# Attention, balanced mixture and routed mixture on one core: small pieces of work dealt out at another spacing among the matrix products

## The chip, the core and the metric

The kernel runs on one core of a Trainium2 chip. The metric is device time in microseconds (us), the median of three runs. The engines of the core work side by side, each through its own instructions in program order: TensorE (PE in the profile), VectorE (DVE), ScalarE (ACT), GpSimd (POOL) and SyncE (SP), whose queue issues most of the DMAs. They wait for each other on semaphores.

## The reference

Three layers follow each other. An attention reads 32 state rows per head and writes both ways (x reads the states, the states read x); its 2176 rows of 512 go into a mixture of eight experts whose weights come from an exponential that is balanced eight times over rows and columns (the Sinkhorn steps); the result goes into a second mixture in which each row takes one expert.

```python
P = np.exp(logits - logits.max())                    # logits = x @ w_gate, 2176 x 8
for _ in range(8):
    P /= P.sum(1, keepdims=True) + 1e-09
    P /= P.sum(0, keepdims=True) + 1e-09
    P *= N / E
for e in range(E):
    out += P[:, e:e+1] * (np.maximum(x @ w1[e], 0.0) @ w2[e])
```

The second mixture picks the largest logit of each row, computes relu(x @ w1[e]) @ w2[e] for the rows of expert e, and scales them by a softmax weight and a sigmoid.

## The kernel before

Everything is float32 in and out; each product is made of three products of a high and a low half (names ending in h and l, hi and lo), and the low half is the difference of the source and its rounded high half.

**The order is written by hand.** The whole program is traced under a manual schedule: each engine executes what concerns it in the order in which the Python code emits it. So a piece of work that is emitted between two groups of products stands there on TensorE too, and if its operand is late, TensorE waits with everything behind it.

**The balanced mixture** is the bulk: three passes over the rows (PASSES: 768, 768 and 640 rows), and in each 32 steps, one for each of eight experts and four quarters of the hidden width (NU = 32, NQ = 4). A step has two halves. `mm1` (L453) makes seven products of six matmuls each by a Strassen-like scheme: seven operands of x (`xop`, written by `xsums` and `xsplit` at the start of a pass) against seven of the weights (`prep_w1`, on ACT and POOL). Its results are added up on DVE, go through relu on ACT, and are split on ACT and DVE into HB. `mm2` (L519) multiplies them tile by tile (6 tiles of 128 rows, 5 in the last pass) with the second weights, six matmuls a tile, and DVE adds each tile, scaled by its balanced weight, to `acc`. The loop emits mm1 of step s and then mm2 of step s-1. In pass 0 the first two experts are added up without their weights, expert 0 in acc and expert 1 in xst (L531 to L539), because the balanced weights PG are not yet there; at step 8 both are brought together with PG (L540 to L543).

**The side work** is dealt out by a queue: `pump(dt)` (L935) is called after each group of six products with 1.04 us (mm1; 0.88 in the last pass) and after each tile of mm2 with 1.36 us, adds that to a credit of at most four paces, and takes one piece off the queue for each `pace` of credit; `flush` (L931) takes all. The queue holds, in pass 0, the attention of batches 2 and 3 (`window`, L947, and the `lag` pieces; 52 pieces with the gates), the logits (`gate`, L292: per row tile of 128, four products of two matmuls each with 8 columns), and the 18 pieces of `sinkhorn` (L311): each `row` has five instructions on DVE, each `col` a matmul of ones (L337) and four on DVE. The attention of batches 0 and 1 (c1 to c5, named A0, A1, C0 and C1 at the top level) stands ahead of the first product.

**At a pass change** (L1057 to L1068) the x operands of the next pass are split in `todo` pieces behind the tiles of the last two mm2, and each finished tile of acc is stored, transposed on TensorE (`final_a`, L552, matmuls pf) and multiplied with the second mixture's gates (`final_b`, L571, matmuls pl). The routing of finished tiles (`route`, L586: fa, fb and fc, matmuls prank; `sel_a` to `sel_c`, matmuls ptab and pgat) is queued at the beginning of the next pass. At the end of the last pass the first weights of the second mixture are split in eight pieces (`split_piece`, L768), and blocks 0 and 1 of it run (`m1`, `hT`, `m2s`) with the last routing among them (L1147 to L1160); the other blocks follow, each with its weights loaded (`load_w`) and split (`split_w`) when the expert changes.

**Banks.** All results of TensorE go to eight rotating banks of PSUM (`bank`, L72). A bank is free again when its readers on DVE or ACT are done, so a late DVE stops TensorE some tiles later.

## Time and profile before

| | us |
|---|---|
| median of 3 runs | 1878.95 |
| the runs | 1878.01 to 1881.89 |
| the profiled execution, its own time | 1879.49 |
| its span, from the first instruction to the last | 1877.8 |
| TensorE busy | 1804.5 |
| VectorE, GpSimd, ScalarE busy | 1211.8, 1099.3, 653.3 |

The span is 1.7 us shorter than the execution's own time, and that execution is 0.5 us over the median. TensorE counts as busy also when its clock is granted at half; the clock has a row of its own in the page's slices. A wait of an engine is listed with the engine and the line that ended it. Where a POOL or DVE instruction is long without more work in it, the same shape elsewhere tells its usual duration.

### The profile page before, as it was taken

What the parts mean: (1) busy time and instruction counts of PE and PEld (TensorE: products, weight loads), DVE (VectorE), ACT (ScalarE), POOL (GpSimd) and SP (SyncE); (2) the same over time, 40 slices, a digit from 0 to 9 for tenths busy, and PEclk for the clock granted to TensorE, in tenths of its full rate; (3) what the DMA queues carried; (4) which work ended last, traced back from release to release, by engine and by line L of the source; (5) the groups of instructions that cost most, each with busy time, mean ns of one, the idle gap of its engine ahead of it and who ended that gap; (6) DMA issues with size and microseconds to landing.
All of it is one profiled execution on the core that took longest, in us unless ns stands there. A gap on an engine that the chain in (4) does not pass through costs nothing.

```text
span 1877.8 us, 25502 instructions
## 1 busy us (share of the span) xinstructions
PE 1804.5 (96%) x9327; PEld 1607.7 (86%) x9327; DVE 1211.8 (65%) x2041; ACT 653.3 (35%) x1114; POOL 1099.3 (59%) x857
## 2 busy tenths in 40 slices
PE   7998899999999999999999999799999999899998
PEld 5997788999999889999999998689999899778886
DVE  5664769666666676666666666896666666745332
ACT  3432222333333333333333333333333343345333
POOL 2432456666776566666667765577787877412212
PEclk8799899999999999999999999899999999999999
DMA  4243112322222222222222222232222222245122
GB/s 113 74 107 96 51 45 68 102 68 68 68 68 68 90 80 71 70 71 96 68 68 68 68 67 84 67 129 81 80 79 79 90 79 68 76 137 199 62 81 89
DMA packets 126618, 154.65 MB, mean 82 GB/s; under 512 B 41424, under 2 KB 91600, under 8 KB 123920
## 3 DMA queue, kind: packets, MB, share of 16 engines
q1 hardware_dynamic: 121920, 142.41, 24.2%
q0 software_dynamic: 3280, 10.23, 1.7%
q8 instruction: 75, 1.23, 0.3%
q14 instruction: 63, 0.52, 0.1%
q10 hardware_dynamic: 1280, 0.26, 0.1%
HBM read 138.99 MB, written 14.42 MB: 82 GB/s over the span
## 4 chain that ended last, share of the span: by engine, by line
PE 74%; DVE 9%; issue 9%; DMA 5%; POOL 2%; ACT 1%; SPq 0%; POOLq 0%; DVEq 0%; ACTq 0%
PE py L527 12%; PE py L528 12%; PE py L529 12%; PE p L465 11%; PE p L467 11%; PE p L466 11%; DMA out_dram<-xst,si 4%; DMA out_dram<-y,si 1%; DVE HB L478 1%; PE psg L303 1%; PE psr L281 1%; PE pss L206 1%; PE pl L576 1%; DVE acc L547 1%; PE pso L243 1%
## 5 line engine op out<-in xcount | busy, mean ns | idle before, releaser
L443 POOL TENSOR_TENSOR wl<-rawb,wh 128x1024 fp32r<-128x1024 f32 x96 | 230.8, 2405 | 473.1 <-ACT wh L442 473.1
L465 PE MATMUL p<-XR 128*128 128x384 f32 (+1 forms) x1344 | 447.9, 333 | 4.2 <-ACT XR L390 2.8
L467 PE MATMUL p<-XR 128*128 128x384 f32 (+1 forms) x1344 | 444.1, 330 | 4.1 <-POOL XR L432 3.0
L466 PE MATMUL p<-XR 128*128 128x384 f32 (+1 forms) x1344 | 443.7, 330 | 0.9 <-DVE XR L392 0.9
L527 PE MATMUL py<-wh,HB 128*128 128x512 f32 x1088 | 431.6, 397 | 2.4 <-DVE acc L547 2.3
L528 PE MATMUL py<-wl,HB 128*128 128x512 f32 x1088 | 429.0, 394 | 0.0
L529 PE MATMUL py<-wh,HB 128*128 128x512 f32 x1088 | 428.6, 394 | 0.0
L547 DVE SCALAR_TENSOR_TENSOR acc<-py,PG,acc 128x512 f32<-128x512 f32 x485 | 338.9, 741 | 79.3 <-PE py L529 78.7
L432 POOL TENSOR_TENSOR XR<-sst,XR 128x1024 fp32r<-128x1024 f32 x96 | 255.0, 2656 | 50.8 <-ACT XR L426 50.8
L465 PEld LDWEIGHTS p<-XR 128*128 128x128 f32 x1344 | 256.8, 191 | 11.3 <-ACT XR L390 4.1
L467 PEld LDWEIGHTS p<-XR 128*128 128x128 f32 x1344 | 256.5, 191 | 5.4 <-POOL XR L432 3.8
L466 PEld LDWEIGHTS p<-XR 128*128 128x128 f32 x1344 | 256.7, 191 | 4.9 <-DVE XR L392 1.5
L478 DVE SCALAR_TENSOR_TENSOR HB<-u,HB 128x384 fp32r<-128x384 f32 (+1 forms) x192 | 169.3, 883 | 117.4 <-ACT HB L474 117.2
L529 PEld LDWEIGHTS py<-wh,HB 128*128 128x128 f32 x1088 | 206.7, 190 | 44.2
L527 PEld LDWEIGHTS py<-wh,HB 128*128 128x128 f32 x1088 | 206.8, 190 | 44.0 <-DVE acc L547 3.0
L528 PEld LDWEIGHTS py<-wl,HB 128*128 128x128 f32 x1088 | 206.6, 190 | 39.7
L483 ACT COPY u<-p 128x384 f32<-128x384 f32 (+1 forms) x96 | 44.3, 461 | 527.6 <-PE p L467 523.5
L428 POOL TENSOR_TENSOR XR<-rawb,XR 128x512 fp32r<-128x512 f32 x96 | 141.6, 1475 | 7.4 <-ACT XR L422 7.4
L426 ACT CAST XR<-sst 128x1024 fp32r<-128x1024 f32 x96 | 100.8, 1050 | 93.7 <-POOL sst L421 93.7
L474 ACT ACTIVATE HB<-u 128x384 fp32r<-128x384 f32 (+1 forms) x192 | 96.9, 505 | 80.0 <-DVE u L501 72.2
L486 DVE TENSOR_TENSOR u<-p,u 128x384 f32<-128x384 f32 (+1 forms) x96 | 51.3, 534 | 112.6 <-PE p L467 108.2
L474 ACT ACTIVATE HB<-p 128x384 fp32r<-128x384 f32 (+1 forms) x96 | 45.5, 474 | 190.4 <-PE p L467 190.4
(292 smaller groups left out, 2491.4 us busy)
## 6 DMA issues: line engine op xcount, KB each, us to landing
rawb<-in_moe_w_dram SPq DMA_DIRECT2D x192, 512.0 KB, 3.5
raw<-in_moe_w_dram SPq DMA_DIRECT2D x15, 1024.0 KB, 6.4
xb<-in_x_dram SPq DMA_DIRECT2D x60, 128.0 KB, 3.1
rawb<-in_moe_w_dram SPq DMA_DIRECT2D x5, 1024.0 KB, 5.1
x1d<-acc SPq DMA_DIRECT2D x16, 256.0 KB, 2.4
xtd<-xtm SPq DMA_DIRECT2D x4, 512.0 KB, 3.0
x1p<-acc SPq DMA_DIRECT2D x8, 256.0 KB, 2.6
xst<-xtd SPq DMA_DIRECT2D x1, 1536.0 KB, 8.3
```

The lines of the kernel that those rows point to most:

```text
L428: nc.gpsimd.tensor_tensor(out=wop(s, 1, 0, 2).rearrange(r, k=KD), in0=raw[:, :, 0:P], in1=wop(s, 0, 0, 2).rearrange(r, k=KD).bitcast(F32), ...
L432: nc.gpsimd.tensor_tensor(out=wop(s, 1, 3, 4), in0=sst.rearrange("p a c -> p (a c)"), in1=wop(s, 0, 3, 4).bitcast(F32), op=ALU.subtract)
L443: nc.gpsimd.tensor_tensor(out=lo, in0=raw, in1=hi.bitcast(F32), op=ALU.subtract)
L465: nc.tensor.matmul(ps, wh, xh, start=start and k == 0, stop=False, skip_group_check=True)
L466: nc.tensor.matmul(ps, wh, xl, start=False, stop=False, skip_group_check=True)
L467: nc.tensor.matmul(ps, wl, xh, start=False, stop=stop and k == 1, skip_group_check=True)
L474: nc.scalar.activation(out=hh[:, f, half * h : (half + 1) * h], in_=c, func=AF.Relu)
L478: nc.vector.scalar_tensor_tensor(out=hl[:, f, q], in0=c, scalar=0.0, in1=hh[:, f, q].bitcast(F32), op0=ALU.max, op1=ALU.subtract)
L527: nc.tensor.matmul(ps, hh[:, j, r], whi[:, j, :], start=(j == 0), stop=False)
L528: nc.tensor.matmul(ps, hh[:, j, r], wlo[:, j, :], start=False, stop=False)
L529: nc.tensor.matmul(ps, hl[:, j, r], whi[:, j, :], start=False, stop=(j == 1))
L547: nc.vector.scalar_tensor_tensor(out=a, in0=ps, scalar=PG[:, t, e : e + 1], in1=a, op0=ALU.mult, op1=ALU.add)
```

## The change

**At the start** the constants are made ahead of the first load's code, and products of ones (`idle_work`: 256 columns of bfloat16 into a bank that nobody reads) are put in five places: 24 ahead of the first transposes, and 3, 3, 4 and 4 further on. **Step 0:** the splits of x are all on DVE (three of seven were on POOL), two of them stand ahead of the end of the attention of batch 1, the others between the products of step 0; the second product of operand 1 comes directly behind the first product, and five single gates stand between products. **Gates** come a tile at a time (17 pieces in place of 6), among the attention pieces. **Pace:** the 59 pieces behind the first five have 132 us of credit in place of 66 for 52. **Three experts apart:** expert 2 is also added up without its weight, in `home[0]` (the buffer that takes the place of the attention's tiles); the balance starts at step 9 in ten pieces with a pace of 5.6, its weights are first used at step 12, and twelve `merge` pieces bring experts 1 and 2 into acc afterwards with a pace of 3.6; the routing constants on POOL follow them (they were at step 9), and the load of the next pass's x goes from step 14 of a pass to step 20. **Pass changes:** a split behind every second tile; final_a two tiles behind its tile, its last six pieces in the next pass's first step; empty pieces (`rest_`) between the routing pieces. **End:** the eight splits are spread over the last ten tiles, the last two on DVE; the routing of the last tile, the block table and the load of block 2's weights go into m1(1), and the table, gather and gate products into m2s(0).

```diff
     def constants():
+        nc.vector.memset(ones, 1.0)
+        nc.vector.memset(onesb, 1.0)
         make_identity(nc, ident)
-        nc.vector.memset(ones, 1.0)
+    def idle_work(n):
+        wide = ones.bitcast(BF)
+        ps = bank("idle")
+        for _ in range(n):
+            nc.tensor.matmul(ps[:, 0 : 2 * P], onesb, wide, start=True, stop=True)
...
     (sinkhorn)
-        steps += [s0, s1]
-        for i in range(8):
-            steps += [row, col(i)]
+        steps += [s0, both(s1, row)]
+        for i in range(7):
+            steps.append(both(col(i), row))
+        steps.append(col(7))
...
-    def xsplit(p, t, order=(0, 4, 3, 5, 1, 2, 6), pool=(3, 1, 6)):
+    def xsplit(p, t, order=(0, 4, 3, 5, 1, 2, 6)):
+        pool = (3, 1, 6) if p > 0 else ()
...
     (mm1)
         nc.scalar.copy(u2, B_[1])
         between(0)
+        if s == 0:
+            prod(2, B_[1], start=False)
+            relu(B_[1], 0, 0)
+            between(4)
+            rest(B_[1], 0, 0)
         new(6)
...
         between(3)
-        prod(2, B_[1], start=False)
+        if s > 0:
+            prod(2, B_[1], start=False)
...   (relu, between(4) and rest of that product likewise only for s > 0)
+    NRAW = 3
+    def apart(e, t):
+        return (xst if e == 1 else home[0])[:, t * DM : (t + 1) * DM]
+    def merge(e, t):
+        a = accv(t)
+        return lambda: nc.vector.scalar_tensor_tensor(out=a, in0=apart(e, t), scalar=PG[:, t, e : e + 1], in1=a,
+                                                      op0=ALU.mult, op1=ALU.add)
...
     (mm2)
-        if p == 0 and e < 2:
-            if e == 1:
-                a = xst[:, t * DM : (t + 1) * DM]
+        if p == 0 and e < NRAW:
+            if e > 0:
+                a = apart(e, t)
...
-        if p == 0 and u == 2 * NQ:
+        if p == 0 and u == NRAW * NQ:
             nc.vector.tensor_scalar_mul(a, a, PG[:, t, 0:1])
-            nc.vector.scalar_tensor_tensor(out=a, in0=xst[:, t * DM : (t + 1) * DM], scalar=PG[:, t, 1:2], in1=a,
-                                           op0=ALU.mult, op1=ALU.add)
...
     (top level, the start)
-        load_x(0, 0)
         constants()
+        load_x(0, 0)
...
         load_raw(0, 1)
+        idle_work(24)
         state_T(0)
         A0[0]()
+        idle_work(3)
         load_x(1, 1)
         A1[0]()
         A0[1]()
+        idle_work(3)
         A1[1]()
...      (idle_work(4) ahead of A0[3] and once more after A1[4])
-        C0[3]()
         C1[2]()
+        C0[3]()
+        sums, T0 = xsums(0, accf)
+        parts = xsplit(0, T0, (0, 1, 4, 3, 5, 2, 6))
+        parts[0]()
         C1[3]()
         C0[4]()
         C1[4]()
+        parts[1]()
         sums[0]()
         sums[1]()
         parts[2]()
...
+        early = {0: [parts[3], sums[2]], 4: [parts[4]], 1: [parts[5], sums[3]], 2: [parts[6]]}
+        def rest_(n):
+            return [lambda: None] * n
...
-            pace[0] = 2.4
+            pace[0] = 5.6
...
     (step_mm1)
             def between(i):
+                if s == 0:
+                    for f in early.get(i, ()):
+                        f()
+                    if i in (0, 4, 1, 2, 3):
+                        queue.pop(0)()
...
-        queue += [gate(range(0, 4)), gate(range(4, 6)), gate(range(6, 8))]
...
+        queue += [gate([t]) for t in (6, 7, 0, 1, 2)] + spread(window(2), [3, 4, 5], 4)
+        queue += spread(window(3), range(8, 12), 3)
...      (spread puts one gate([t]) behind every n pieces; tiles 12 to 15 likewise between the lag pieces)
-        pace[0] = 66.0 / len(queue)
-        queue += [close_reads] + sinkhorn()
+        queue += [seq(gate([NT - 1]), states_out), close_reads]
+        pace[0] = 132.0 / (len(queue) - 5)
+        credit[0] = -7.3
+        balance = sinkhorn()
...
     (step loop)
-            if s == 9:
-                flush()
-                routing_constants()
-            if p < 2 and u == 14:
+            if p < 2 and u == 20:
                 xload(p + 1)
...
-                queue += list(Rq[0])
+                queue += [Rq[0][0]] + rest_(2) + [Rq[0][1]] + rest_(1) + [Rq[0][2]]
                 pace[0] = 3.0
...
-                queue += [Rq[1][0], seq(Rq[1][1], sel_a), Rq[1][2], Rq[2][0], sel_b, sel_c, Rq[2][1], load_first, first_rows, Rq[2][2]]
+                queue += [Rq[1][0]] + rest_(2) + [seq(Rq[1][1], sel_a)] + rest_(2) + [Rq[1][2], Rq[2][0]] + rest_(1) + [
+                    sel_b] + rest_(2) + [sel_c, load_first, Rq[2][1], first_rows, Rq[2][2]]
...
+                if s == 2 * NQ + 1:
+                    flush()
+                    queue += balance
+                if s == NRAW * NQ + 1:
+                    flush()
                 if u > 0:
                     step_mm2(s - 1)
+                if s == NRAW * NQ + 1:
+                    queue += [merge(e, t) for e in range(1, NRAW) for t in tiles_of(0)] + [routing_constants]
+                    pace[0] = 3.6
...
     (last step of pass 0 and 1)
-                todo += xsplit(p + 1, T0)
+                for f in xsplit(p + 1, T0):
+                    todo += [f, None]
+                del todo[11]
                 step_mm2(s - 1)
-                hooks = {ts[i]: [A[ts[i - 1]]] + ([Bq[ts[i - 2]]] if i > 1 else []) for i in range(1, 6)}
-                step_mm2(s, hooks)
+                a, b = [A[t] for t in ts], [Bq[t] for t in ts]
+                step_mm2(s, {ts[2]: [a[0]], ts[3]: [a[1]], ts[4]: [b[0], a[2]], ts[5]: [b[1], a[3]]})
...
-                queue += [seq(A[ts[5]], Bq[ts[4]]), Bq[ts[5]]]
-                pace[0] = 2.0
+                queue += [b[2], a[4], b[3], a[5], b[4], b[5]]
+                pace[0] = 1.0
...
     (last step of pass 2)
-                for i in (2, 3, 0, 1):
-                    todo.append(lambda i=i: split_piece(SETS[0], i, 1024, nc.gpsimd))
-                todo.append(lambda: load_first_raw(1, 1))
+                piece = [lambda i=i: split_piece(SETS[0], i, 1024, nc.gpsimd if i < 6 else nc.vector) for i in range(8)]
+                todo += [piece[2], seq(piece[3], lambda: load_first_raw(1, 1)), piece[0], None, piece[1], None, piece[4], None, piece[5]]
...
-                step_mm2(s, {13: [A[12]], 14: [A[13], Bq[12]], 15: [A[14], Bq[13]], 16: [Bq[14], A[15], lambda: xT(0)]})
-        for i in range(4, 8):
-            split_piece(SETS[0], i, 1024, nc.gpsimd)
+                step_mm2(s, {13: [A[12]], 14: [A[13], Bq[12]], 15: [A[14], Bq[13]],
+                             16: [piece[6], Bq[14], A[15], piece[7], lambda: xT(0)]})
...
     (the second layer's first blocks)
-        m1(0, (seq(A[16], Rq[3][0]), seq(Bq[15], Bq[16]), seq(Rq[4][0], Rq[3][1]), Rq[4][1]))
+        m1(0, (seq(A[16], Rq[3][0]), seq(Bq[15], Bq[16]), seq(Rq[4][0], Rq[3][1])))
         xT(1)
-        blocks()
-        load_w(2, 0)
-        m1(1, (None, lambda: hT(0), btab))
-        gather(2)
-        Rq[3][2]()
-        Rq[4][2]()
-        gmul()
-        m2s(0)
+        m1(1, (seq(Rq[4][1], blocks, lambda: load_w(2, 0)), lambda: hT(0)))
+        m2s(0, (None, btab, lambda: gather(2), seq(Rq[3][2], Rq[4][2], gmul)))
```

## Rows read from the trace of the kernel before

**Rows 1.** the page's parts 1 and 2: busy time, then tenths in 40 slices

```profile
PE 1804.5 (96%) x9327; PEld 1607.7 (86%) x9327; DVE 1211.8 (65%) x2041; ACT 653.3 (35%) x1114; POOL 1099.3 (59%) x857
...
PE   7998899999999999999999999799999999899998
...
PEclk8799899999999999999999999899999999999999
```

**Rows 2.** stretches of the run: length, busy time of engines (instructions), clock, DMA

```profile
0.00:40.50 40.50, 29.22 (x132) 23.70 (x132) 18.56 (x37) 15.77 (x29) 7.82 (x13) 0.87 0.42 97
40.50:70.20 29.70, 27.46 (x109) 26.16 (x110) 15.58 (x21) 8.38 (x14) 12.58 (x10) 0.54 0.34 92
70.20:192.40 122.20, 115.58 (x707) 102.64 (x706) 77.30 (x146) 43.60 (x94) 42.24 (x33) 0.96 0.37 98
192.40:261.70 69.30, 58.07 (x254) 49.22 (x253) 55.49 (x123) 16.08 (x28) 29.38 (x24) 0.88 0.15 46
...
312.50:328.00 15.50, 15.50 (x79) 14.06 (x78) 14.37 (x22) 5.16 (x9) 10.67 (x9) 1.00 0.21 69
629.90:692.00 62.10, 54.01 (x271) 48.05 (x270) 43.52 (x74) 21.17 (x36) 33.74 (x24) 0.89 0.29 99
...
1174.00:1248.00 74.00, 62.11 (x350) 56.28 (x351) 64.35 (x147) 23.41 (x46) 45.93 (x39) 0.91 0.30 99
...
1598.00:1658.00 60.00, 53.24 (x290) 44.25 (x288) 43.68 (x120) 23.43 (x32) 24.67 (x14) 0.94 0.42 144
```

**Rows 3.** TensorE's waits, whole run: total us, times, longest

```profile
PE pscol L337 <- DVE sm L332: 11.2, 6, 3.7
PE prank L628 <- DVE oh L612: 9.9, 3, 4.1
PE pf L565 <- DVE acc L547: 6.7, 2, 4.0
PE psst L166 <- DMA stp<-in_state_dram: 6.0, 1, 6.0
PE psb L272 <- DVE e L266: 4.7, 2, 3.6
PE pgat L681 <- DVE osg L739: 4.6, 1, 4.6
...
PE p L465 <- ACT XR L390: 2.8, 2, 1.5
PE py L527 <- DVE acc L547: 2.3, 2, 1.4
```

**Rows 4.** the timeline of the start (start us, us, engine, line, operation)

```profile
11.14 6.93 PE L206 MATMUL pss<-sbd,xT 128*128 128x64 f32 x32
...
21.70 1.91 PE L206 MATMUL pss<-sbd,acc 128*128 128x64 f32 x16
...
40.52 0.96 DVE L392 TENSOR_TENSOR XR<-xst,XR 128x768 fp32r<-128x768 f32 x1 [0.25 <-ACT XR L390]
...
47.78 6.12 PE L303 MATMUL psg<-wg,xst 128*128 128x8 f32 x28
```

**Rows 5.** the balance: its tiles alone by engine; one of its lines

```profile
193.00:262.00 69.00, 3.90 (x18) 3.14 (x18) 27.86 (x75) 0.41 (x1) 0.00 (x0) 0.88 0.15 46
...
L340 DVE TENSOR_SCALAR sm<-sm x8: 171/174/2297, 207.0 to 255.8; 128x8 f32<-128x8 f32 x8
```

**Rows 6.** timelines of DVE and POOL: step 8's merge, and the end of the passes

```profile
288.25 2.62 DVE L541 TENSOR_SCALAR acc<-acc,PG 128x512 f32<-128x512 f32 x1
290.91 0.75 DVE L542 SCALAR_TENSOR_TENSOR acc<-xst,PG,acc 128x512 f32<-128x512 f32 x1
...
287.88 2.71 POOL L432 TENSOR_TENSOR XR<-sst,XR 128x1024 fp32r<-128x1024 f32 x1
...
1618.77 2.35 DVE L610 TENSOR_TENSOR rt_v<-rt_v,rev 128x24 f32<-128x24 f32 x1
...
1618.67 9.38 POOL L773 TENSOR_TENSOR XR<-raw,XR 128x1024 fp32r<-128x1024 f32 x4 [8.69 <-ACT XR L772]
```

More of the change, by code (lines that the diff above doesn't have):

```diff
@@ L493, in mm1 @@
         between(3)
-        prod(2, B_[1], start=False)
+        if s > 0:
+            prod(2, B_[1], start=False)
         tt(out=c22, in0=B_[5], in1=u3, op=ALU.add)
-        relu(B_[1], 0, 0)
+        if s > 0:
+            relu(B_[1], 0, 0)
         relu(c22, 1, 1)
-        between(4)
+        if s > 0:
+            between(4)
         new(3)
-        rest(B_[1], 0, 0)
+        if s > 0:
+            rest(B_[1], 0, 0)
         tt(out=u4, in0=B_[3], in1=u4, op=ALU.add)
@@ L878, in tile_state_attention_moe_moe2 @@
                 crit[b, g], lag[b, g] = attention(b, g)
+        constants()
         load_x(0, 0)
-        constants()
         load_state(0)
@@ L902, in tile_state_attention_moe_moe2 @@
         C0[1]()
+        idle_work(4)
         A0[3]()
@@ L961, in window @@
                     c[1], n20, e[1], c[2], n21, e[2], c[3], nx(0, n30), e[3],
-                    nx(1, n31), c[4], e[4], gate(range(4 * b, 4 * b + 4))]
-        home = [None]
+                    nx(1, n31), c[4], e[4]]
         def close_reads():
@@ L1015, in step_mm2 @@
                 if todo:
-                    todo.pop(0)()
+                    f = todo.pop(0)
+                    if f is not None:
+                        f()
                 pump(1.36)
```

36 lines of the change are left out of this document (19 added, 17 removed).

## Prediction

> **What bounds the kernel now.** I read the page first. TensorE is busy for 96% of the span and DVE, the next, for 65% [rows 1], so TensorE sets the end; the question is where it runs at full pace. Its slices fall below 9 at four places: the first six slices, the 14th, the 25th and 26th, and the 35th, and the clock's slices fall at nearly the same places [rows 1]. So I asked next for the stretches around them. In the undisturbed one a step takes 15.50 us with 79 matmuls at clock 1.00 and no idle time [rows 2]; it is the kernel's floor, and agrees with the code's own credits (7 x 1.04 + 6 x 1.36 = 15.4). The change leaves these steps alone. What it can win lies in the disturbed stretches, in two parts: TensorE's idle time, whose causes the list of waits names [rows 3], and the time at half clock, which costs length x (1 - clock). From the stretches [rows 2]: 29.7 x 0.46 = 13.7 us in step 0, 122.2 x 0.04 = 4.9 in the attention behind it, 69.3 x 0.12 = 8.3 in the balance, 62.1 x 0.11 = 6.8 at the first pass change, 74.0 x 0.09 = 6.7 after the second, 60.0 x 0.06 = 3.6 at the end; together 44. In the first 40 us the printed 0.87 is too good: 32 matmuls pss took 6.93 us from 11.14, 0.217 us each, and 16 of the same shape 1.91 from 21.70, 0.119 each [rows 4]; the first were at the half level of 1.2 GHz. The reader is to see that each clock loss stands with a wait or with a run of tiny matmuls: in step 0, 28 gate matmuls of 8 columns follow each other for 6.12 us [rows 4], and TensorE counts as busy in them.
>
> **The change part by part** (bounds in brackets, all in us won).
>
> Start, to 40.5. The 24 products of ones lie in the 6.0 us in which TensorE waits for the states [rows 3]; 256 columns are two thirds of a 384-column product (1.04 / 6 = 0.174 at full clock), so some 0.12 each, at half clock 0.23, 5.6 in all: hidden, with 0.4 to spare; 14 more cost 1.6 to 3.2 where TensorE is not waiting anyway. If they bring the full clock, the 32 pss above save 3.5, but the chain behind goes through DVE and through x loads that are issued as late as before. I take 1.5 [-0.5 to 3.5], by the chain rather than the matmuls.
>
> Step 0, 40.5 to 70.2. At full clock its work is 7 x 1.04 = 7.3 for products, 64 gate matmuls at half of 6.12 / 28, 7.0, and about 1 of attention: 15.4, and 14.3 is lost. Afterwards 24 of the gate matmuls come later (no gain). What is late next is DVE: seven splits, four sums (0.96 each [rows 4]) and ten of mm1's own at about 0.5 are 16, against 11.7 of TensorE work, so at full clock some 4.4 stays lost, and at half clock 11.7. Gain between 14.3 - 11.7 = 2.6 and 9.9. Single gates between six products make runs of tiny matmuls a quarter as long, and two products no longer wait for the end of the attention (the 2.8 us on ACT XR [rows 3]). I take 7.5, nearer the upper end.
>
> The Trainium skill, "TensorE: Matmul & The Clock Gate", part 4, says that transposes on TensorE do not count as busy for the full clock. Here the clock rose at 21.7 us after a stretch in which TensorE did little but transposes, so the trace speaks against it; by the page the start stays at half clock wherever the products of ones do not reach, which is the second rival's start.
>
> Attention of batches 2 and 3, 70.2 to 192.4. 132 us of credit for 59 pieces is 2.2 us a piece in place of 66 / 52 = 1.3. The waits to go: psb on DVE 4.7, and about 2 of the smaller ones [rows 3], with 4.9 of clock; the half clock there follows the long runs of gate matmuls, which are split. At most 11.6; switching between small pieces stays. I take 9 [4 to 12].
>
> Balance and merge, 192.4 to 303. To go: pscol on DVE 11.2, py on acc 2.3 [rows 3], behind step 8's merge (one tile's instructions there are 2.62, 0.75 and another addition, where a tile of mm2 takes TensorE 1.36 [rows 6]), and 8.3 of clock: 22 in all. What is late next is again DVE. The balance is 75 instructions and 27.9 us of it; at L340's usual 0.17 (once it took 2.30) they would be 13 [rows 5]. Before, DVE was busy for 55.5 of 69.3 [rows 2]. Now ten pieces at 5.6 are 56 us, with a base of about 10 a step (55.5 less 27.9 for three steps), 36 to 40: 49 to 68. So 0 to 12 of DVE's time finds no room; banks cover part, and I take 4 lost. The twelve merges are six more two-operand instructions of 0.75 than before, spread over 43 us: nothing, while DVE has room; behind each stand the additions that free banks. I take 16 [8 to 22]. An added wait: the first write to expert 2's buffer must wait until the attention's last store has left the same space; DVE's queue stands behind it, and eight banks of 1.36 cover about 10 us. Nothing.
>
> Here a rule speaks against the change: the Trainium skill, "SBUF — State Buffer", "Who interferes with whom", lets a DVE instruction with two SBUF inputs and a GpSimd instruction that reads SBUF not run together; the later one waits for all of the other. The trace agrees: L541 took 2.62 beside a POOL instruction of 2.71 [rows 6]. By it, each of the twelve merges costs DVE up to 2.7 more; that is the first rival.
>
> First pass change, 629.9 to 692. To go: pf on DVE 4.0, a prank of 4.1 [rows 3] and 6.8 of clock, 14.9. final_a two tiles (2.7) later and fewer splits on DVE ahead of it end the first; seven us of products between fa and fb end the second. The last split, on POOL, is needed only by the last product of the next step, over 6 us later. I take 12 [7 to 14.5]. Second change: pf 2.7 (the rest of 6.7), prank 3.4, pgat 4.6 [rows 3], 6.7 of clock and some 2 of smaller waits, 19; the spacing is the same in kind. I take 14 [8 to 18].
>
> End, 1598 to 1658. To go: prank 2.5 (the rest of the 9.9 [rows 3]), about 2.6 of smaller waits, 3.6 of clock: 8.7. POOL's splits at 1618.67 held DVE (2.35 for 24 columns [rows 6]); they come earlier. But the routing of the last tile and the block table now start inside m1(1), and load_w(2,0) with its two megabytes hangs on them: that chain may be late for m1(2). I take 5 [0 to 8].
>
> Loads moved from step 14 to 20 are needed four steps, 62 us, later: nothing. The eleven added gate pieces are the same matmuls: nothing. The 14 later products of ones: -2.
>
> Sum: 1.5 + 7.5 + 9 + 16 + 12 + 14 + 5 - 2 = 63. The profiled execution took 1879.5; 1879.5 - 63 = 1816. It lies 0.5 over the median, which changes nothing.
>
> **The rivals.** First, DVE takes TensorE's place where the balance and merges are. The balance keeps its 27.9 us of DVE, the twelve merges cost 2 more each (24), and half of that reaches TensorE: 4 + 12 more lost than forecast, and step 0 at 4 instead of 7.5: 1816 + 20 = 1836. For it: DVE was already at 80% in the old balance [rows 2]; against: the pieces are 5.6 apart. Second, the clock stays low at the start: start and step 0 at their lower ends, -0.5 + 2.6 in place of 9, and 4 less in the attention: 1827; it shares the forecast's range. Third, nearly everything goes: the upper ends sum to 88, less 2: 1794. Fourth, the waits travel with the pieces: what is late is DVE's queue, not the piece's neighbour, so each wait on DVE [rows 3] stays; then only the clock in step 0 and half the attention are won, 12, 1868. Fifth, slower: small pieces mixed over 9 steps thin out TensorE's work so that the half level holds from the start to the end of step 9, about 170 us of work at full clock. That adds up to 170; it decides from 126 us at half clock, where 63 are lost and the sum is nothing; at the whole it is 1816 + 170, at 150 us some 1891. Against it: the old attention had its pieces closer, and its stretch shows 0.96 [rows 2].
>
> **How the numbers follow.** Forecast with the second rival 0.62, first 0.17, third 0.09, fourth 0.05, fifth 0.04, and 0.03 for a change that does about nothing. 1816 is the likeliest; 1796 to 1844 holds the forecast's bounds, the first two rivals and part of the third. 0.2% (3.8 us) is about what a measurement of this kernel can tell from no change: faster 0.93, same 0.03, slower 0.04.
>
> **What would show it.** After: step 0's products ending about 15 us after their start; clock 1.00 through the attention; no pscol, psb or pf among the waits over 1 us; DVE over 90% busy from step 9 to 12 with TensorE still at 9 or more tenths; the second block's m1 some 5 us nearer to the last mm2. Wrong would be waits of TensorE on acc (L547) in steps 9 to 16, half clock in the first 60 us, or m1(2) waiting on a split.

## The result and the profile after

| | us |
|---|---|
| before, median of 4 runs | 1880.42 (1878.01 to 1882.70) |
| changed, median of 4 runs | 1846.74 (1844.86 to 1849.35) |
| ratio, 95% interval | 0.9822 (0.9802 to 0.9842) |
| profiled execution of the changed kernel, its span | 1845.63, 1843.4 |

The change wins 34 us where 63 were forecast; the time lies 2.7 above the range's upper end. The page of the changed kernel (busy times, then tenths in 40 slices), against [rows 1]:

```profile
PE 1787.8 (97%) x9365; PEld 1594.5 (86%) x9365; DVE 1219.0 (66%) x2064; ACT 653.2 (35%) x1114; POOL 1086.4 (59%) x851
...
PE   7899998999999999999999999999999999899998
...
PEclk8799999999999999999999999999999999899999
```

The slices of the two pass changes are filled, and so is the attention; step 0 (the second slice), the balance (the seventh) and the end (the 35th) are not. The stretches of the changed kernel that answer to [rows 2], in order: step 0; steps 1 to 8 with the attention; steps 9 to 13 with the balance; the first pass change; the second; the end (columns: length, busy time and instructions of each engine, granted clock, DMA share and rate):

```profile
39.80:69.20 29.40, 20.67 (x85) 20.55 (x84) 16.80 (x28) 9.60 (x16) 9.08 (x7) 0.60 0.36 95
69.20:241.20 172.00, 170.85 (x1006) 153.06 (x1004) 123.62 (x219) 62.79 (x125) 82.01 (x65) 1.00 0.33 92
241.20:338.00 96.80, 87.18 (x451) 78.53 (x450) 80.44 (x159) 27.46 (x51) 48.60 (x40) 0.96 0.18 58
600.00:693.00 93.00, 90.86 (x480) 81.76 (x479) 71.66 (x120) 34.64 (x60) 58.56 (x44) 0.98 0.28 94
1108.00:1240.00 132.00, 123.51 (x697) 110.46 (x696) 106.84 (x215) 46.32 (x87) 86.73 (x69) 0.99 0.31 104
1554.00:1624.00 70.00, 62.06 (x330) 52.65 (x328) 42.05 (x128) 25.55 (x36) 22.46 (x14) 0.93 0.36 125
```

And what TensorE waited for, over the whole run (total, times, longest), against [rows 3]:

```profile
PE pscol L344 <- DVE sm L339: 9.6, 4, 5.2
PE p L481 <- ACT u L499: 8.7, 1, 8.7
PE p L483 <- POOL XR L448: 8.1, 7, 2.3
PE pY L882 <- DVE HB L873: 4.0, 2, 3.7
```

pf and psb are gone, and of prank and pgat next to nothing is left; pscol is nearly as before (11.2). Two waits are new, on ACT's copy of u2 and on hT(0), and the one on POOL's low halves of weights has grown (L432 in the kernel before: 3.0, 3 times, longest 1.8). To place the gain, I take the start of the first product of a step in both traces (steps count from 0 to 95; the differences of these starts are free of what follows):

| stretch | before | changed | won | forecast |
|---|---|---|---|---|
| start to step 0 | 40.5 | 39.8 | 0.7 | 1.5 - 2 |
| step 0 to step 1 | 30.5 | 29.4 | 1.1 | 7.5 |
| step 1 to 18: attention, balance, merges | 350.1 | 331.9 | 18.1 | 25 |
| step 31 to 36: first pass change | 100.3 | 90.2 | 10.1 | 12 |
| step 63 to 95: second pass change | 450.5 | 442.6 | 7.9 | 14 |
| step 95 to the end | 285.7 | 289.3 | -3.6 | 5 |

Steps 18 to 31 take 201.6 in both, and 36 to 63 agree as well. What a stretch loses I estimate as its length less its matmuls, each at the pace that its form shows at full clock (0.173 us for 384 columns, 0.227 for 512, 0.11 for the small ones). In the attention that is about 15 before and 4 after; in the steps behind it up to 18, with the balance and the merges, 26 and 15. Some 4 us of matmuls came to these steps from step 0 (24 of the gates and ten transposes). So the 18.1 are about 7 for the attention and 11 for the balance and the merges. Step 0 gave these 4 us away and became only 1.1 shorter: it loses more than before, 17.6 in place of 14.9. Four terms missed by 5 to 9 us each: step 0, the balance, the second pass change, the end. The experiments take them in this order; each is the changed kernel with the edit shown, and its starts of steps are compared with the changed kernel's.

### The profile page after: what moved, and what is told of

The parts are those of the page before. It is cut to its first block, busy times and chain, and to the rows that moved or that the text cites. A ratio compares the mean times of both kernels' runs of the same rounds, so it can differ in the third digit from the quotient of the medians.

```text
span 1843.4 us, 25573 instructions
## 1 busy us (share of the span) xinstructions
PE 1787.8 (97%) x9365; PEld 1594.5 (86%) x9365; DVE 1219.0 (66%) x2064; ACT 653.2 (35%) x1114; POOL 1086.4 (59%) x851
## 4 chain that ended last, share of the span: by engine, by line
PE 71%; issue 12%; DVE 8%; DMA 4%; POOL 3%; ACT 1%; SPq 0%; POOLq 0%; DVEq 0%; ACTq 0%
PE py L563 12%; PE py L564 12%; PE py L565 12%; PE p L481 10%; PE p L483 10%; PE p L482 10%; DMA out_dram<-xst,si 2%; DVE HB L494 1%; DMA out_dram<-y,si 1%; DVE acc L581 1%; POOL XR L448 1%; PE psr L288 1%; PE pss L213 1%; POOL wl L459 1%; PE psg L310 1%
## 5 line engine op out<-in xcount | busy, mean ns | idle before, releaser
L581 DVE SCALAR_TENSOR_TENSOR acc<-py,PG,acc 128x512 f32<-128x512 f32 x461 | 321.2, 740 | 63.3 <-PE py L565 62.6
L483 PEld LDWEIGHTS p<-XR 128*128 128x128 f32 x1344 | 255.6, 190 | 11.7 <-POOL XR L448 10.1
L494 DVE SCALAR_TENSOR_TENSOR HB<-u,HB 128x384 fp32r<-128x384 f32 (+1 forms) x192 | 186.7, 974 | 111.5 <-ACT HB L490 111.2
L563 PEld LDWEIGHTS py<-wh,HB 128*128 128x128 f32 x1088 | 204.4, 188 | 44.5 <-DVE u L507 3.0
L565 PEld LDWEIGHTS py<-wh,HB 128*128 128x128 f32 x1088 | 204.2, 188 | 43.4
```

Source lines behind the costliest of these rows:

```text
L483: nc.tensor.matmul(ps, wl, xh, start=False, stop=stop and k == 1, skip_group_check=True)
L494: nc.vector.scalar_tensor_tensor(out=hl[:, f, q], in0=c, scalar=0.0, in1=hh[:, f, q].bitcast(F32), op0=ALU.max, op1=ALU.subtract)
L563: nc.tensor.matmul(ps, hh[:, j, r], whi[:, j, :], start=(j == 0), stop=False)
L565: nc.tensor.matmul(ps, hl[:, j, r], whi[:, j, :], start=False, stop=(j == 1))
L581: nc.vector.scalar_tensor_tensor(out=a, in0=ps, scalar=PG[:, t, e : e + 1], in1=a, op0=ALU.mult, op1=ALU.add)
```

## The experiments

**Step 0: the wait on ACT.** First TensorE from the end of the first product, then ACT in the same time (start, us, the instruction, idle time before it):

```profile
40.80 0.34 PE L483 MATMUL p<-XR 128*128 128x384 f32 x1
40.98 0.95 PE L310 MATMUL psg<-wg,xtm 128*128 128x8 f32 x8
50.66 0.69 PE L481 MATMUL p<-XR 128*128 128x384 f32 x1 [8.73 <-ACT u L499]
```

```profile
44.25 0.83 ACT L406 CAST XR<-acc 128x768 fp32r<-128x768 f32 x1 [2.94 <-DVE acc L392]
46.38 3.71 ACTq L145 DMA_DIRECT2D stp<-in_state_dram  x8
50.13 0.48 ACT L499 COPY u<-p 128x384 f32<-128x384 f32 x1 [5.05 <-DMA stp<-in_state_dram]
```

The second product writes into the first one's bank, and so must wait for the copy of u2; on ACT that copy stands behind a cast that waits for a sum on DVE, and behind eight DMA issues. (The issues themselves begin only when DVE, at 46.07, clears the tile that they fill.) The kernel before had the same issues in front of the same copy, but there the next products write other banks, the second one comes late in the step, and TensorE waits for none of it:

```profile
53.29 3.66 ACTq L137 DMA_DIRECT2D stp<-in_state_dram  x8
57.00 0.48 ACT L483 COPY u<-p 128x384 f32<-128x384 f32 x1 [4.01 <-DMA stp<-in_state_dram]
```

The first experiment moves the issues to another queue.

```diff
-            nc.scalar.dma_start(out=stp[...], in_=sv[q])
+            (nc.scalar if b < 2 else nc.sync).dma_start(out=stp[...], in_=sv[q])
```

> The changed kernel with one edit: the eight loads of the states of batches 2 and 3 are issued by SP's queue, no longer by ACT's. Nothing is left out. In the changed kernel the second product waits 8.88 us (41.9 to 50.7) on ACT's copy of u2 (L499 at 50.13), and ACT's list of the seconds before it holds an x cast, then eight DMA issues that took 3.71 us from 46.38. Theory A, the issues are the delay: the copy comes at about 46, the wait falls to some 5 us or less, and because less idle time precedes it the half clock of 45.6 to 69.5 shrinks; step 1's first product comes 4 to 14 us earlier (55 to 65 in place of 69.18), and the end moves with it (1832 to 1842). Rival B, the copy is late because DVE is (the casts and splits that ACT takes turns with): the wait stays over 6 us and step 1 begins within 2 us of 69.18.

The wait fell from 8.7 to 3.6 and step 1 came 5.8 earlier (63.4); 6.0 was won at the end of the trace, and the median is 1841.42. Theory A, at the lower end of its numbers: what is left of the wait is the cast behind DVE's sum, and step 0 stayed at half clock from 42.7 to 63.2. The Trainium skill, "DMA: Bandwidth & Descriptors", "Issuing engines are not separate DMA queues", says that issuing on several engines saves only issue time, usually small beside the DMA itself. Beside the DMA it is small here too (0.46 us an issue, 2.0 from issue to landing); but the trace shows where it counts all the same: eight issues, 3.71 us together, stand in front of an instruction for which TensorE waits.

The next run fills what remains of that wait.

```diff
                     if i in (0, 4, 1, 2, 3):
                         queue.pop(0)()
+                    if i == 0:
+                        idle_work(30)
```

> The state loads on SP's queue, as in the first experiment, and 30 products of ones behind the first gate piece of step 0, that is, inside TensorE's wait for the u2 copy (3.58 us there, 41.5 to 45.1; 30 products of 256 columns are some 3.2 us at full clock). Nothing is left out. With the states on SP step 0 took 24.0 us, of which 10.2 went to half clock (42.7 to 63.2). Theory A, the clock falls because of that wait: with it filled the clock stays at full through step 0, whose products then go on DVE's and ACT's pace, and step 1's first product comes at 54 to 59 in place of 63.4; the end 4 to 9 us earlier than with the states on SP alone (1828 to 1833). Rival B, the clock falls because of what lies before (the chain of the last attention pieces from 30 to 40, small matmuls with waits): half clock from about 43 all the same, step 1 at 62 to 64, no gain, the filling lost in the wait.

Step 0 of the first experiment, and of this one:

```profile
39.40:63.40 24.00, 20.42 (x84) 20.30 (x83) 16.38 (x26) 9.36 (x16) 9.08 (x7) 0.57 0.45 116
```

```profile
39.30:58.90 19.60, 17.19 (x115) 15.60 (x113) 16.90 (x28) 8.65 (x15) 8.42 (x7) 0.91 0.45 115
```

The clock of the stretch is 0.91 in place of 0.57, and it fell only at 55.5, in the second of two further waits (0.5 and 1.1). Theory A as to the clock: it was the wait that took it, not the small matmuls ahead of it. Step 1 came 10.3 earlier than in the changed kernel, 4.5 earlier than with the states on SP alone. For the end theory A fails: it had 1828 to 1833, the median is 1840.57, and in the trace only 6.7 of the 10.3 was left, 0.7 more than without the filling: 0.9 went in steps 1 to 8, 1.0 in step 13, and 1.9 behind the first pass change, where TensorE now waits 1.9 on acc (L579), which the changed kernel, at half clock shortly before, did not. The last two losses are not shown to come from the filling: the first two runs on the end below, whose edits lie far behind these places, have them too (step 13 took 24.1 and 24.2 there and 24.2 here, in the changed kernel 23.2; steps 31 to 36 took 92.1 in all three and 90.2), with the same wait on acc. So one trace can differ from the next by some 3 us at these places.

**The products of ones at the start.**

```diff
-        for _ in range(n):
+        for _ in range(min(n, 1)):
```

> The changed kernel with one product of ones at each of the five places in place of 24, 3, 3, 4 and 4. Nothing of the computation is left out. It asks what the products of ones are worth, whose clock was forecast to bring about 1.5 us and to cost 2. Theory A, they buy little: step 0's first product within 1.5 us of 39.83, the end within 3 us of the changed kernel's. Rival B, they hold the clock up where it is up (4.7 to 11.5, 21.7 to 28.6, 35.4 to 45.6): without them the transposes and pss run at half, and step 0 begins 3 us or more later.

Step 0 began at 39.64 (39.83 with all of them), and the end came 0.7 later in the trace, 1848.64 by the median. Theory A: at the start they are worth nothing that can be told from none. But the 3.5 that the forecast named for full clock in the products pss was not put to the test. With all of them the clock is full from 4.7 to 11.5 and at half again when the 32 products pss begin; the first half of these takes 3.48, and 3.52 without products of ones:

```profile
11.46 3.48 PE L213 MATMUL pss<-sbd,xT 128*128 128x64 f32 x16
```

What full clock there would be worth is not shown.

**The balance.** Two runs thin out DVE's list in different ways; both change the output, and each was executed once. The first leaves POOL without work (and ACT without the casts of w2):

```diff
+        quiet = 10 <= s <= 14
...
+            if not quiet:
                 nc.gpsimd.tensor_tensor(...)       # the sums and low halves of w1
...
+        if 9 <= s <= 13:
+            W2[s] = W2[8]
+            load_raw(s + 1, 1)
+            return
```

> The changed kernel without GpSimd's work on the weights of steps 10 to 14 (sums, the low halves of w1) and without w2's casts and low halves in steps 9 to 13 (those steps use step 8's w2); the output is not the reference's for that. ACT's casts of w1 and all loads stay. It asks what makes DVE late in the balance. In the changed kernel the stretch from step 9's start (241.15) to step 14's (337.99) is 96.8 us, against 77.5 for five undisturbed steps, so 19.3 lost, with pscol waits of 9.6 and DVE busy 75.0 of 85 us from 253. Theory A, DVE is late because single instructions of it take long beside POOL's (L494 on u 1.51 us mean against 0.55 for its other forms, L336 0.82 against about 0.2): without POOL's work DVE's busy time there falls to about 60, the pscol waits fall below 2 us and the stretch to 78 to 84 us. Rival B, the balance's chain is simply too long for one pace (dependent steps on DVE at 5.6 us each behind the additions), whatever POOL does: the waits stay over 6 us and the stretch over 90.

The second takes out half of the balance:

```diff
-        for i in range(7):
+        for i in range(3):
             steps.append(both(col(i), row))
-        steps.append(col(7))
+        steps.append(col(3))
...
-            pace[0] = 5.6
+            pace[0] = 10.0
```

> The changed kernel with four of the balance's eight rounds left out and the six remaining pieces at a pace of 10.0 in place of ten at 5.6; the output is not the reference's for that. GpSimd's work stays. It thins out DVE's list by about 11 us and leaves everything else. Theory A (DVE's list is full, from whatever causes): the pscol waits fall below 2 us and the stretch from step 9's to step 14's start falls from 96.8 to 78 to 85 us. Rival B (what costs is the single collision of a piece with a long GpSimd instruction, not the density): waits of 1.5 us or more remain at half or more of the four rounds, and the stretch stays over 88 us.

Steps 9 to 13 without POOL's work, and with four rounds (the changed kernel's row stands above, 241.20:338.00):

```profile
241.30:325.50 84.20, 84.20 (x451) 76.87 (x450) 65.08 (x162) 22.77 (x46) 0.00 (x0) 1.00 0.18 60
```

```profile
240.70:324.00 83.30, 83.30 (x443) 76.01 (x442) 65.20 (x117) 27.70 (x51) 49.20 (x40) 1.00 0.22 67
```

In both, DVE's time falls from 80.4 to 65, all pscol waits go, the clock holds at 1.00, and the stretch falls from 96.8 to 84 and 83: theory A twice, though with four rounds 2.7 was lost again in step 14, under the merges. (The stretch's own floor is five steps of 15.50 and some 5 us of the attention's last pieces, 82.) Which instructions grow beside POOL: the low half of the hidden layer and a column of 17 elements in the changed kernel, and both without POOL's work (the first is L502 there; by shape: total, mean ns):

```profile
L494 DVE SCALAR_TENSOR_TENSOR HB<-u,HB 128x384 fp32r<-128x384 f32 x10 | 15.1, 1512 | 2.2 <-ACT HB L490 2.2
...
L336 DVE TENSOR_SCALAR sm<-sm 128x17 f32<-128x17 f32 x8 | 6.5, 815 | 0.3
```

```profile
L502 DVE SCALAR_TENSOR_TENSOR HB<-u,HB 128x384 fp32r<-128x384 f32 x10 | 5.5, 555 | 2.7 <-ACT HB L498 2.7
...
L336 DVE TENSOR_SCALAR sm<-sm 128x17 f32<-128x17 f32 x8 | 1.4, 177 | 0.3
```

1512 ns beside POOL and 555 without are 9.6 of the 15 us that DVE got back, 815 and 177 another 5.1. The means hide two kinds: in the changed kernel five of the ten low halves took 0.55 to 0.63 us, and the other five 2.42 to 2.48, each begun 0.4 behind a POOL instruction of 2.4:

```profile
253.77 2.42 DVE L494 SCALAR_TENSOR_TENSOR HB<-u,HB 128x384 fp32r<-128x384 f32 x1 [0.38 <-ACT HB L490]
```

```profile
253.38 2.39 POOL L448 TENSOR_TENSOR XR<-sst,XR 128x1024 fp32r<-128x1024 f32 x1 [2.21 <-ACT XR L442]
```

This is the rule cited in the prediction from the Trainium skill, "SBUF — State Buffer", "Who interferes with whom"; the trace agrees with it here too, and shows it as a load of 2 us a step more than as a stop of TensorE. The column of 17 elements has one input in SBUF, which the rule as the prediction has it leaves out; it took 0.18 us by itself and up to 2.33 beside POOL.

An edit that leaves nothing out, with a second one for the routing of the last pass:

```diff
             if q == 0:
-                nc.vector.tensor_copy(a, ps)
+                nc.scalar.copy(a, ps)
...
-                nc.vector.tensor_scalar_mul(cr, cr, float(N) / E)
-                nc.vector.tensor_tensor(out=PG, in0=PG, in1=cr..., op=ALU.mult)
+                nc.vector.scalar_tensor_tensor(out=PG, in0=PG, scalar=float(N) / E, in1=cr..., op0=ALU.mult, op1=ALU.mult)
...
-                pace[0] = 4.0       # routing behind the second change
+                pace[0] = 8.0
```

> The changed kernel with three edits for DVE's list. The six copies of each first quarter of experts 0 to 2 are made by ACT in place of DVE; the balance's column scale is one instruction shorter a round (the factor goes into the multiplication with PG); and the pieces of the routing after the second pass change stand 8.0 apart in place of 4.0. Nothing is left out. If DVE's full list is what costs in the balance (steps 9 to 13, 96.8 us, 14.8 lost) and after the second pass change (1108 to 1240, 13.0 lost): some 6 us less of DVE work in the balance take the stretch to 86 to 92 us with pscol waits under 5, and the wider pace takes 4 to 7 us out of the second stretch (waits on XR L448 and L444 and on u L507, 8.2 together, under 3); the end at 1828 to 1836. Rival: six us of 75 do not open DVE's list (the pieces still come at 5.6), the balance stays above 94; and the waits on XR after the second change stay, because they come from the pass change's own splits on POOL and not from the routing; the end at 1843 or later.

The balance came to 94.4 with 6.0 of pscol waits, which is the rival's; the second change won 1.4, where the theory had 4 to 7, and the median is 1842.00, just ahead of the rival's 1843. DVE's time in the balance fell by 7.8, to 72.6, and that does not empty the list at this pace; at the second change waits on XR of 5.4 stayed (1.2, 2.4 and 1.9), so the first two at least, right behind the change, are not owed to the routing's spacing.

**The pass changes: POOL's list.** POOL behind the second one, in the new pass's first step, which has seven products (6.2 us) and no second layer (start, us, idle time before; four sums of 0.74 and one low half left out):

```profile
1144.06 2.37 POOL L459 TENSOR_TENSOR wl<-rawb,wh 128x1024 fp32r<-128x1024 f32 x1 [4.90 <-ACT wh L458]
...
1149.30 1.52 POOL L444 TENSOR_TENSOR XR<-rawb,XR 128x512 fp32r<-128x512 f32 x1
...
1151.72 2.58 POOL L448 TENSOR_TENSOR XR<-sst,XR 128x1024 fp32r<-128x1024 f32 x1
```

10.2 us without a gap, for weights which the next step's products want from 1149.3 on.

```diff
-            nxt = prep_w1(s + 1) if s < LAST else [lambda: None] * 2
+            nxt = prep_w1(s + 1) if s < LAST and s not in (NU, 2 * NU) else [lambda: None] * 2
...
                 del todo[11]
+                todo[5], todo[9] = prep_w1(s + 2)
```

> The changed kernel with one move at each of the two pass changes: the first-layer weights of the new pass's second step are prepared beside the second layer of the old pass's last two steps, where POOL shows 8.5 and 4.9 us without work (1129.1 to 1137.6, 1139.2 to 1144.1), in place of the new pass's first step, which has only seven products (6.2 us) and in which POOL works from 1144.06 without a gap to 1154.3. Nothing is left out. Theory A, that list of POOL's, which does not fit in the short step, is what is late behind the pass changes: the waits on XR L448 and L444 there (2.30 at 643; 1.32 and 2.51 at 1150) go, with one half-clock stretch each, 3 to 4 us won at the first change and 4 to 6 at the second; the end 5 to 9 us earlier. Rival B, DVE sets the pace there through u and the casts on ACT: TensorE waits on u or acc for the same 2 to 4 us, and the end moves by less than 2.

These waits went, and with them the half clock at both changes: 2.4 won at the first (3 to 4 expected; TensorE then waits 1.9 on acc L579), 4.0 at the second; 1838.74 by the median; 7.3 at the end of the trace, 0.7 of it from an earlier start. Theory A, a little under its numbers. Rows of both changes, full clock throughout:

```profile
600.00:690.00 90.00, 88.14 (x478) 79.80 (x477) 70.57 (x120) 34.81 (x60) 58.68 (x43) 1.00 0.29 94
1105.00:1236.00 131.00, 124.28 (x711) 111.22 (x709) 106.61 (x217) 48.27 (x91) 88.25 (x70) 1.00 0.32 105
```

**The end.** TensorE in m2s(0), and DVE's list ahead of it: the first and the last instruction of the block table, then the low half for which TensorE waits:

```profile
1604.22 0.50 PE L882 MATMUL pY<-XR,HB 128*128 128x512 f32 x1 [3.67 <-DVE HB L873]
```

```profile
1596.77 0.29 DVE L1149 TENSOR_TENSOR sm<-prank,k 128x136 f32<-128x136 f32 x1
...
1603.42 0.15 DVE L1187 TENSOR_SCALAR flag<-sm 128x1 int32<-128x1 f32 x1
1603.49 1.28 DVE L873 TENSOR_TENSOR HB<-pt,HB 128x512 fp32r<-128x512 f32 x2
```

Three runs change this order.

```diff
-        m1(1, (seq(Rq[4][1], blocks, lambda: load_w(2, 0)), lambda: hT(0)))
+        m1(1, (Rq[4][1], seq(lambda: hT(0), blocks, lambda: load_w(2, 0))))
```

> The changed kernel with one edit at the end: in the first hook of the second block's m1 only the last routing piece is left; the block table and load_w(2,0) go into the second hook, behind hT(0). Nothing is left out. In the changed kernel TensorE waits 3.83 us for hT(0)'s low half, whose subtraction on DVE (1604.18) stands behind routing and block table, and the clock is at half from 1605.5 to 1612.3. Theory A, the order on DVE is what costs: the wait goes, and with it the half clock or most of it; the distance from m1(1)'s first product to m1(2)'s first falls from 31.04 to 24 to 27 us, and the end comes 4 to 7 us earlier (1839 to 1842). Rival B, the load of the third block's weights is the limit behind it: the distance stays within 1.5 us of 31.04, and m1(2) or a matmul close to it waits on a split or on a load.

m1(1) to m1(2) took 29.6 in place of 31.0, and 1848.11 by the median. By its length this is rival B, but the cause is neither theory's: TensorE no longer waited for hT(0), but 2.2 for the table itself, and the clock went to half for as long as before.

```profile
PE ptab L715 <- DVE sm L1176: 2.2, 1, 2.2
```

So the table's product was put later as well:

```diff
-        m2s(0, (None, btab, lambda: gather(2), seq(Rq[3][2], Rq[4][2], gmul)))
+        m2s(0, (None, seq(Rq[4][2], gmul), None, None, None, btab, lambda: gather(2)))   # Rq[3][2]: m1(0)'s last hook; m1(1) as above
```

> The changed kernel with the end put in another order: hT(0) ahead of the block table on DVE, as in the second experiment, and besides the table's product five rows of m2(0) later, the last factors of the routing ahead of it (one of them in m1(0)'s last hook) and the gates' products sooner. Nothing is left out. In the second experiment TensorE waited 2.25 us for the table in place of 3.83 for hT(0), and the clock was at half for the same 6.8 us, so the end gained nothing. Theory A, each of these waits is one of order on DVE, and without them the clock holds: m1(1) to m1(2) falls from 31.04 to 25 to 28. Rival B, the third block's weights are next: their load is issued at 1609.4 in the second experiment (1604.4 in the changed kernel), and loads, casts and low halves of its first half took until 1623: the distance stays at 28.5 or above and m1(2) or pxg(2) waits on a split or on the gather.

m1(1) to m1(2) 28.0, but m1(2) to m1(3) 12.0 where the changed kernel has 7.9, and 1850.24 by the median. The length is the upper end of theory A's, the cause is rival B's: the loads of the third block were issued at 1611.3 (1604.4 in the changed kernel), ACT waited for them (2.52 and 1.99), and m1(2) ran behind them, at clock 0.72. The last run goes back to the order before the change:

```diff
-        m1(0, (..., seq(Rq[4][0], Rq[3][1])))
+        m1(0, (..., seq(Rq[4][0], Rq[3][1]), Rq[4][1]))
         xT(1)
-        m1(1, (seq(Rq[4][1], blocks, lambda: load_w(2, 0)), lambda: hT(0)))
-        m2s(0, (None, btab, lambda: gather(2), seq(Rq[3][2], Rq[4][2], gmul)))
+        blocks()
+        load_w(2, 0)
+        m1(1, (None, lambda: hT(0), btab))
+        gather(2)
+        Rq[3][2](); Rq[4][2](); gmul()
+        m2s(0)
```

> The changed kernel with the last lines' order (m1(0) to m2(0)) as the kernel before had it; all else as changed. Nothing is left out. From the last first-layer product of step 95 to m1(2) the kernel before took 65.9 us (1592.1 to 1658.0) and the changed one 69.9 (1554.1 to 1624.1), where the forecast had 5 won. Theory A, the new order of these lines is what lost it: with the old order m1(1) to m1(2) falls from 31.04 to 25 to 27 (24.9 before), and the stretch to 64 to 67, the end 3 to 6 us earlier. Rival B, the loss comes from what lies before them (the splits and routing moved into the last step), and only changes its place: the stretch stays within 1.5 us of 69.9.

m1(1) to m1(2) in the changed kernel and with the old order:

```profile
1593.00:1624.00 31.00, 26.70 (x130) 22.16 (x130) 21.42 (x76) 8.40 (x9) 5.81 (x6) 0.89 0.47 170
```

```profile
1593.80:1618.00 24.20, 23.16 (x126) 19.33 (x126) 19.36 (x68) 8.46 (x9) 5.81 (x6) 1.00 0.59 213
```

24.2 in place of 31.0, no wait for hT(0) and no half clock. In the old order, too, the block table stands ahead of hT(0)'s low half on DVE; but it begins 1.0 behind m1(1)'s first product (1593.75), not 3.8 as in the changed kernel, because the last tile's ranks (Rq[4][1]) come in m1(0):

```profile
1594.72 0.29 DVE L1149 TENSOR_TENSOR sm<-prank,k 128x136 f32<-128x136 f32 x1
...
1601.42 1.28 DVE L873 TENSOR_TENSOR HB<-pt,HB 128x512 fp32r<-128x512 f32 x2
```

Step 95 to m1(2) is 62.3, where it was 65.9 before the change and 69.9 after. Theory A: the new order of these lines lost 7.6, and the rest of the change at the end won 3.6. By the median the gain is smaller, 2.9 (1843.82); the profiled execution is the fastest of its four runs.

**Together.** The edits of the filled wait, of the lighter DVE list (the balance at a pace of 6.0) and of the early weights in one kernel, and then the old end with them:

> The changed kernel with the edits of four experiments together: states on SP and 30 products of ones in step 0's wait; first quarters copied by ACT, the shorter column scale and the balance at a pace of 6.0; the wider pace of the routing; the early weights at both pass changes. Nothing is left out. If the parts add, as theirs are different stretches: 10 in step 0, 3 to 6 in the balance, 5 to 9 at the pass changes, 1.5 in the routing, 19 to 26 in all: 1818 to 1827. Rival: the half clock takes part of it back, as in the run with the filled wait, where step 1 came 10.3 earlier and the end 6.7: 1827 to 1834.

> The joined kernel with the old order of the end as well (m1(0) to m2(0) as in the kernel before). Nothing is left out. The joined kernel came 22.5 earlier than the changed one, and the old order alone took 7.3 out of the end (m1(0) to m1(2) 43.4 in place of 36 there). Theory A, these terms belong to different stretches and add: m1(1) to m1(2) at 24 to 25, the end 7 earlier, 1814 to 1818. Rival B, the weights of the third block are next as soon as the end comes earlier: the stretch from m1(0) to m1(3) shrinks by less than 4, 1818 to 1822.

1822.31, ratio to before 0.9677 (0.9653 to 0.9700); and 1817.92, ratio 0.9667 (0.9649 to 0.9684). The joined kernel is at its first theory: 9.7 in step 0 (7.2 kept), 6.4 in the balance, 2.4 and 6.7 at the pass changes. The last edit brought 4.4 by the medians (4.6 in the traces) of the 7 expected: 1817.92 is the edge of theory A's range, and m1(1) to m1(2) took 24.3 as it has it, but m1(0) to m1(1) grew by 2.3, with clock 0.76 there, which neither theory had. Its page:

```profile
PE   7999999999999999999999999999999999999998
...
PEclk8899999999999999999999999999999999999999
```

The kernel before was measured again beside every round of runs, with medians from 1879.5 to 1885.1; two or three us between the medians of different rounds can therefore not be told from none, and the ratios to before are the safer comparison (the last column is the end of the trace against the changed kernel's):

| run | median | ratio, 95% interval | earlier |
|---|---|---|---|
| changed | 1846.74 | 0.9822 (0.9802 to 0.9842) | |
| states on SP | 1841.42 | 0.9794 (0.9778 to 0.9810) | 6.0 |
| and the wait filled | 1840.57 | 0.9777 (0.9748 to 0.9806) | 6.7 |
| no products of ones | 1848.64 | 0.9821 (0.9792 to 0.9851) | -0.7 |
| lighter DVE list | 1842.00 | 0.9784 (0.9755 to 0.9813) | 4.9 |
| early weights | 1838.74 | 0.9768 (0.9743 to 0.9793) | 7.3 |
| end, first order | 1848.11 | 0.9825 (0.9809 to 0.9842) | -1.6 |
| end, second order | 1850.24 | 0.9824 (0.9793 to 0.9856) | -3.7 |
| old end | 1843.82 | 0.9796 (0.9772 to 0.9820) | 5.7 |
| joined | 1822.31 | 0.9677 (0.9653 to 0.9700) | 22.5 |
| joined, old end | 1817.92 | 0.9667 (0.9649 to 0.9684) | 27.1 |

Of the single edits only the early weights' interval lies clear of the changed kernel's, and the two joined kernels' intervals overlap. What a single edit is worth rests on its own stretch in the traces. For the end's two new orders the last column misleads: from step 95 on the first is 1.7 shorter than the changed kernel and the second 0.7 longer; 2.9 of what they lost went in steps 13 and 31 to 36, as said above.

## Why the prediction missed

**Right.** The attention (about 7 of 9; clock 1.00, as said), the first pass change (10.1 of 12, pf and prank gone), the products of ones (nothing either way), and the reading that clock and waits go together.

**Step 0 (7.5 taken, 1.1 measured, under its bound of 2.6).** The failed step is "What is late next is DVE". It summed DVE's instructions and not ACT's list: the u2 copy that the earlier second product needs stood behind a cast on DVE's pace and behind eight DMA issues, which the kernel before also had, but with nothing of TensorE's waiting behind them. The price at step 1 has two parts, both shown: 5.8 for the issues and the clearing that they wait for, 4.5 more for the clock that the remaining wait took. Of the second 3.9 still stood at step 9, and 0.7 at the end of that trace.

**Balance (16 taken with the merges, about 11 measured).** The failed step is one term of the sum, "I take 4 lost", too small: steps 9 to 13 lost 14.8, and the two ways of thinning DVE's list brought 12.6 and 13.6 back. DVE's 80.4 us are 83% of the stretch as it ran, but 98% of the 82 that TensorE needs for it; at 72.6 us (89%) 12.4 were still lost, at 65 (79%) one or two. So the sign "DVE over 90%" fails when it is read from a stretch that has already grown. How much of the loss is due to the amount, how much to the pieces' spacing, which four rounds changed as well, is not shown. The first rival names the mechanism, DVE in TensorE's place, but puts 12 of its 16 on the merges, 2 more us each. They took 13.2 in all (least, middle and most in ns):

```profile
L552 DVE SCALAR_TENSOR_TENSOR acc<-xst,PG,acc x6: 736/1222/2305, 341.4 to 356.2; 128x512 f32<-128x512 f32 x6
L552 DVE SCALAR_TENSOR_TENSOR acc<-raw,PG,acc x6: 734/770/1584, 358.8 to 375.6; 128x512 f32<-128x512 f32 x6
```

That is about 4 more than twelve of the shortest, and steps 14 to 17 lost about 1. That its 16 lies near the 14.8 is luck.

**Second pass change (14 taken, 7.9 measured).** "pf 2.7, prank 3.4, pgat 4.6" did go; the failed step is "the spacing is the same in kind", with nothing said of what these waits had hidden: 10.2 us of POOL in a step of seven products. (A wait of 1.1 on it stood there before the change too, L428 at 1184.) Moving that gave 4.0 here and 2.4 at the first change; wider routing pieces 1.4. What remains of the gap, under 1 us, was not taken apart.

**End (5 taken, -3.6 measured).** The chain was named, but its wrong member: "may be late for m1(2)" meant the loads, and they were in time. What was late was hT(0), behind a table of 6.7 us on the same engine, which the change let begin 2.8 later within m1(1). The lower bound of 0 was too high.

**The range.** It does not hold "the forecast's bounds", as the prediction says: the lower ends of its terms add up to 27, which is 1852, not 1844. The 34 measured lie above these 27, though step 0, the end and, by 0.1, the second pass change lie below their own.

Against "What would show it": clock 1.00 through the attention came; step 0's products ended 29 us after their start, not 15; pscol stayed among the waits over 1 us; the second block's m1 came 2.2 nearer, not 5; half clock in the first 60 us was the sign named for a miss, and it came, from another cause than the second rival's.

## What to carry to other kernels

When a wait is removed, write down the whole list of every in-order engine for the time that it covered, DMA issues among it, and ask which entry the next instruction of the bound engine now needs. A gap of a few us on TensorE can cost twice, once as the wait and once as the clock behind it. Work that nobody reads gave the clock back inside such a gap here, and brought nothing ahead of the first real work. Look for a gain at its own stretch and at the end of the program: later stretches take some of it back or vary by themselves. Judge how full an engine's list is by the time that the bound engine needs for the stretch, not by the time that the stretch took. An order at the end that looks late can be the one in which three chains just meet: try it by itself.

## What the runs showed of the hardware

In a wait of 8.7 us in step 0 the clock fell to half (1.2 GHz), from 45.6 to 69.5. With the wait cut to 3.6 us the granted clock of the stretch was 0.57, and with products of ones in that time 0.91. Eight DMA issues on ACT took 3.71 us, 0.46 each, and held its next computing instruction for as long. A DVE instruction of 0.55 us with two inputs in SBUF took 2.42 to 2.48 beside a POOL instruction of 2.39 to 2.45; one of 0.18 us with one input took up to 2.33.
